# Matmuls on 64 by 32 array tiles issued in pairs, two PSUM tiles at a time, in a planned attention and SMELU kernel

## The chip, the cores and the metric

One core of one Trainium2 chip. The metric is device microseconds of one execution. The kernel before was timed three times: 260.14, 260.56 and 262.5 us, median 260.56.

## The reference

Two chained softmax attentions, then a two-layer network with a piecewise quadratic activation. Batch 8, 8 heads, 576 tokens, head size 64, 32 packed queries per head, d_ff 2048.

```python
def sm_attn(qq, kk, vv):
    s = scale * np.matmul(qq, kk.transpose(0, 1, 3, 2))
    s = s - np.max(s, axis=-1, keepdims=True)
    a = np.exp(s)
    a = a / (np.sum(a, axis=-1, keepdims=True) + 1e-09)
    return np.matmul(a, vv)
p_packed = sm_attn(p, k, v)
out = sm_attn(q, p_packed, p_packed)
...
h = x @ w_in
g = np.where(h >= 1, h, np.where(h <= -1, 0.0, (h + 1) ** 2 / 4))
return g @ w_out
```

## The kernel before

The work is split by batch b = 0 to 7; the output is made by pairs of batches, 1152 tokens in 9 tiles of 128 rows.

For each batch, `attention(b, key)` adds these steps. `trans` turns k and q: in batches 0 to 2 TensorE transposes them (`tp`, L359) and ScalarE or VectorE copies them into `kT` and `qT`; from batch 3 on `turned` (L479) does it with transposing transfers issued by SyncE, one for each half of the heads (parts 0 and 1). `scores` (`sp`, L387) multiplies kT with the packed queries pT, one PSUM tile for each half, and ScalarE takes the exponential (`ex`). `packed` (`pk`, L407 and L412) makes the packed values and their sums; they are copied into `ppT`. `weights(g, ...)` makes the second scores for one of two groups of heads: eight matmuls on 64 by 32 tiles of the array (`s`, L433, 288 columns), then exp (`eT`), sums over 32 rows by a matmul (`sm`, L443), ln and exp (`ln`, `rc`) and the product `A` (L454). `mk(f, ...)` makes a quarter of `M`, the packed values times w_in: eight matmuls on 64 by 32 tiles (`mp`, L473, 512 columns), copied out by ScalarE or VectorE.

Then `hidden_tile(b, fi)` (`h`, L513) multiplies M and A into a 128 by 576 tile, four matmuls, 16 tiles for each batch; ScalarE and VectorE apply the activation (`x`) and write `hT`. `out_tile(pr, i)` (`o`, L556) adds up 16 matmuls of 512 columns for each of the nine tiles of a pair; the result is copied to `ob` and SyncE writes it out (L562). All four kinds of engine work share 3 PSUM tiles ("W", `psW`), and o has 2 of its own ("O").

Nothing runs as it is written down. `Plan.run` is a list scheduler that runs when the kernel is built: each step has a cost for each engine (dictionary `C`), a key (its urgency), dependencies, and the PSUM room that it takes. For each engine `choose` takes the most urgent step that can start within half of the best candidate's cost after that candidate. The order that comes out is the program order of each engine. The plan's costs say 3.0 us for a load of k, q or v and 5.0 us for a transposing transfer. `mode` marks steps whose tiling of the array differs: 0 for the whole array, 1 for pk, 2 for s and mp; a step in another mode costs `switch` more.

SyncE's queue carries the transposing transfers and the output rows in one order. GpSimd's queue carries the loads; a load of k, q or v for batch b + 2 waits until the batch b buffer has been read.

Until the first output tiles, TensorE runs matmuls of zeros (L618) where the plan has a gap.

Of the kernel before, what the change touches and what calls it, by code (L numbers as in the profile page):

```python
# [9 lines left out]


C = dict(load=3.0, w_in=2.65, w_out=2.55, out=9.0, p=3.1, land=1.9, xt=5.0, xland=2.5,
         tpp=0.06, tp=0.042, sc=0.034, pk=1.18, s2=0.25, sm=0.245, M=0.345, h=0.49, o=0.217, switch=0.05,
         pTc=0.1, Tca=1.12, Tcd=0.76, Tc2a=0.64, Tc2d=0.457, ex=0.82, ppTa=0.26, ppTd=0.293, rs=0.18, eT=0.74, ln=0.65, rc=0.68, A=0.82,
         Mca=1.0, Mcd=1.22, x=0.65, ta=0.683, td=0.457, hT=0.758, oba=0.585, obd=0.69,
         array=0.2, wake=2.0, tell=0.04, feed=0.1, slack=0.6, margin=0.15, wait=0.5)
# [5 lines left out]
class Task:  # L22

    def __init__(self, engines, cost, key, deps, fn, takes, readers, frees, mode, slack, after, holds):
        self.engines, self.cost, self.key, self.deps, self.fn = engines, cost, key, list(deps), fn
        self.takes, self.readers, self.frees, self.mode = takes, readers, frees, mode
        self.slack, self.after, self.holds = slack, after, holds
        self.users, self.end, self.slot, self.gone = [], None, None, 0.0


class Plan:
# [15 lines left out]
    def add(self, engines, cost, key, deps, fn, takes=None, readers=0, frees=None, mode=None, slack=None, after=0.0,  # L47
            holds=0.0):
        engines = (engines,) if isinstance(engines, str) else engines
        t = Task(engines, cost if isinstance(cost, dict) else {e: cost for e in engines}, key, deps, fn, takes, readers,  # L50
                 frees, mode, slack, after, holds)
        t.seq = len(self.tasks)
        self.tasks.append(t)
        return t

    def ready(self, t, e):
        at = 0.0
        for d in t.deps:
            if e == "PE":
                lag = 0.0 if d.on == "PE" else C["feed"] + (C["margin"] if t.slack is None else t.slack)  # L60
            else:
                lag = C["array"] if d.on == "PE" else C["tell"] if d.on != e else 0.0
            at = max(at, d.end + lag)
        if t.takes:
            room = self.rooms[t.takes][self.count[t.takes] % len(self.rooms[t.takes])]
            if room is None:
                return None
            at = max(at, room + (C["feed"] if e == "PE" else 0.0))
        return at

    def choose(self, e, given, waiting):
# [37 lines left out]
    def run(self, idle):  # L109
        self.line = [t.seq for t in self.tasks if t.engines == ("DMA",)]  # L110
        left = {}
        given = {e: [] for e in self.ENGINES}
        for t in self.tasks:
            left[t] = len(t.deps)
            for d in t.deps:
                d.users.append(t)
            if not t.deps:
                for e in t.engines:
                    given[e].append(t)
        n = len(self.tasks)  # L120
        while n:
            best = None
            for e in self.ENGINES:
                c = self.choose(e, given, n)
                if c is not None and (best is None or c[0] < best[0]):
                    best = c[0], e, c[1]
            if self.count["O"] < 3:
                c, step = self.choose("PE", given, n), DW / 2400
                self.now["PE"] = max(self.now["PE"], C["wake"])
                if (c is None or c[0] > self.now["PE"] + step) and best is not None and best[0] > self.now["PE"]:  # L130
                    idle()
                    self.now["PE"] += step
                    continue
            assert best is not None
            at, e, t = best
            t.on = e
            cost = t.cost[e]
            if e == "PE" and t.mode is not None and t.mode != self.mode:
                cost += C["switch"]
                self.mode = t.mode  # L140
            self.now[e] = at + cost
            t.end = at + cost + t.after + (C["land"] if e == "DMA" else 0.0)
            if e == "DMA":
                del self.line[0]
            self.log.append((at, at + cost, e, t))
            if t.takes:
                room = self.rooms[t.takes]
                t.slot = self.count[t.takes] % len(room)
                room[t.slot] = None
                self.count[t.takes] += 1  # L150
                if t.readers == 0:
                    room[t.slot] = t.end + t.holds
            if t.frees is not None:
                f = t.frees
                f.gone = max(f.gone, t.end)
                f.readers -= 1
                if f.readers == 0:
                    self.rooms[f.takes][f.slot] = f.gone
            if len(t.engines) > 1:
                t.fn(e)  # L160
            elif e in ("ACT", "DVE"):
                t.fn(e)
            else:
                t.fn()
            for x in t.engines:
                given[x].remove(t)
            for u in t.users:
                left[u] -= 1
                if left[u] == 0:
                    for x in u.engines:  # L170
                        given[x].append(u)
            n -= 1
# [3 lines left out]
def kernel(  # L176
# [27 lines left out]
    G = 2  # L204
# [7 lines left out]
    FW = 512  # L212
    NF = d_ff // FW
# [56 lines left out]
    L = {}  # L270
# [31 lines left out]
    def both(fns, cost_a, cost_d, key, deps, **kw):  # L302

        return add((DVE, ACT), {ACT: cost_a, DVE: cost_d}, key, deps, fns, **kw)
# [35 lines left out]
    def attention(b, key):  # L340
# [36 lines left out]
        def scores(i, deps):  # L377
            box, ky = {}, key["sc" + str(i)]

            def mm():  # L380
                sp = box["sp"] = wide([P, 2, FW], f32, "sp")
                for j in range(2):
                    for e in range(E):
                        for g in range(G):
                            h, o = G * (2 * i + j) + g, (e * G + g) * X * NP
                            w = ((G * j + g) * E + e) * TP
                            nc.tensor.matmul(sp[:, j, o:o + X * NP], kT()[:, i, w:w + P],  # L387
                                             pT[:, b, h].rearrange("p x n -> p (x n)"), start=True, stop=True)

            def ev(eng):  # L390
                nc.scalar.activation(ex().rearrange("p e g x a n -> p a (e g x) n")[:, 2 * i:2 * i + 2],  # L391
                                     box["sp"][:TP, :, :E * G * X * NP].rearrange("p j (c n) -> p j c n", n=NP),
                                     AF.Exp, scale=scale)
            t = add(PE, C["sc"] * 12, ky, deps, mm, takes="W", readers=1, mode=0)
            return t, add(ACT, C["ex"], ky, [t] + old("pk"), ev, frees=t)

        def packed(deps):
            box, ky = {}, key["pk"]

            def mm():  # L400
# [9 lines left out]
                for g in range(G):  # L410
                    for c in range(NC):
                        nc.tensor.matmul(s_[:, g], ex_[:, c // X, g, c % X].rearrange("p a n -> p (a n)"), ones2[:TP],  # L412
                                         start=(c == 0), stop=(c == NC - 1))
            t = add(PE, C["pk"], ky, [L["v", b, 0]] + deps, mm, takes="W", readers=4, mode=1)
            war = old("s2", "M")
            res = [both(lambda eng: copy(ppT()[:, 0], box["v"])(eng), C["ppTa"], C["ppTd"], ky, [t] + war, frees=t)]
            for x in range(X):
# [8 lines left out]
        def weights(g, deps, r):  # L426
# [26 lines left out]
            def norm(eng):  # L453
                nc.vector.scalar_tensor_tensor(A()[:, g], box["eT"], rs()[:, g, :1], box["rc"], ALU.mult, ALU.mult)  # L454
            p_ = K.get((b - 1, "A" + str(g)), [])
            t = add(PE, C["s2"], ky, deps, mm, takes="W", readers=1, mode=2)
            e_ = add(ACT, C["eT"], ky, [t, r] + p_, exp2, frees=t)
            t2 = add(PE, C["sm"], km, [e_], mm2, takes="W", readers=1, mode=0)
            l_ = add(ACT, C["ln"], km, [t2] + last.get("ln", []), ln, frees=t2)
            i_ = add(ACT, C["rc"], km, [l_] + p_, inv)  # L460
            a_ = add(DVE, C["A"], km, [i_] + K.get((b - 2, "h"), []), norm)
            last["ln"] = [i_]
            K[b, "A" + str(g)] = [a_]
            return t, e_, a_

        def mk(f, deps):
            box, ky = {}, key["M" + str(f)]

            def mm():
                mp = box["mp"] = wide([P, G, FW], f32, "mp")  # L470
                for a in range(Q):
                    for g in range(G):
                        nc.tensor.matmul(mp[a * NP:(a + 1) * NP, g], pp_of(g, g, a),  # L473
                                         w_in_sb[g * D:(g + 1) * D, a, f * FW:(f + 1) * FW], start=True, stop=True)
            t = add(PE, C["M"], ky, deps + [L["in", f]], mm, takes="W", readers=1, mode=2)
            return t, both(lambda eng: copy(M()[:, :, f * FW:(f + 1) * FW], box["mp"])(eng),
                           C["Mca"], C["Mcd"], ky, [t] + K.get((b - 2, "h"), []), frees=t)

        def turned(nm, i, dst, prev):  # L479
            def go():  # L480
# [13 lines left out]
        pk, pc, r = packed([e0, e1])  # L494
        K[b, "sc"], K[b, "pk"] = [s0, s1], [pk]
        K[b, "kt"], K[b, "qt"] = [k0, k1], [q0, q1]
        ws = [weights(g, pc + qc0 + qc1, r) for g in range(G)]
        ms = [mk(f, pc) for f in range(NF)]
        K[b, "s2"], K[b, "M"] = [w[0] for w in ws], [m[0] for m in ms]
        K[b, "eT"], K[b, "A"] = [w[1] for w in ws], [w[2] for w in ws]  # L500
        K[b, "Mc"] = [m[1] for m in ms]
# [147 lines left out]
```

## Time and profile before

| what | value |
|---|---|
| median of three runs | 260.56 us |
| profiled execution | 261.9 us, span 259.8 us |
| TensorE busy | 247.3 us, 95% |
| VectorE / ScalarE busy | 173.3 us, 67% / 185.9 us, 72% |
| HBM read / written | 37.22 MB / 9.44 MB |
| mean granted TensorE clock | 0.995 |

The span runs from the first to the last instruction. PE is TensorE, PEld its weight loads, ACT ScalarE, DVE VectorE, POOL GpSimd, SP SyncE; a q behind a name is the engine's sequencer, which issues transfers. In a list in order of time a row gives the start, the time from the first start to the last end, the line, what is written and read, and the number of instructions; in square brackets stands the idle time before it and what ended it. In the table by stretches of time the columns are the stretch, its length, then busy time and number of instructions of PE, PEld, DVE, ACT and POOL, the granted clock, the share of the DMA engines and GB/s. A landing row gives the time from a transfer's issue to its landing.

### The profile page before, as it was taken

Reading aid. Unit: us, or ns where it says so; the run is one execution under the profiler, and the core shown is the slowest. Engines: PE = TensorE matmul, PEld = TensorE weight load, DVE = VectorE, ACT = ScalarE, POOL = GpSimd, SP = SyncE. Lnnn points to the kernel's source line nnn. Section 1 sums busy time; section 2 is a strip of 40 time slices with the busy share of each in tenths; the row PEclk is TensorE's granted clock in tenths of the full one; section 3 lists DMA queues with packets and bytes.
Section 4 is the critical chain, followed back from the end, with each engine's and each line's share of the span. In section 5 each row is a group of like instructions: output and inputs, shape, how many; then the busy total and the mean of one; then the engine's idle time right before and its main releaser. Section 6 shows DMA issues by size and latency. Waiting matters only on the chain.

```text
span 259.8 us, 5951 instructions
## 1 busy us (share of the span) xinstructions
PE 247.3 (95%) x2432; PEld 145.7 (56%) x2466; DVE 173.3 (67%) x299; ACT 185.9 (72%) x303; POOL 27.4 (11%) x40
## 2 busy tenths in 40 slices
PE   7999989999998999999999999999999999999992
PEld 5978546467545655654655565555554465644440
DVE  5135989678988997999748974897268876940000
ACT  3447886789898898999949895998559775841110
POOL 8522312102100300210201000000000000000000
PEclk9999999999999999999999999999999999999997
DMA  7999999999999999999999995301222111133223
GB/s 108 187 204 206 208 202 195 217 230 194 139 148 196 148 226 183 178 164 179 161 165 141 154 217 122 76 19 31 43 81 43 42 43 40 40 78 85 59 63 82
DMA packets 54764, 34.40 MB, mean 132 GB/s; under 512 B 27473, under 2 KB 50257, under 8 KB 54737
## 3 DMA queue, kind: packets, MB, share of 16 engines
q0 software_dynamic: 24608, 18.55, 51.7%
q1 hardware_dynamic: 29968, 15.34, 33.4%
q8 instruction: 19, 0.31, 0.5%
q10 hardware_dynamic: 160, 0.13, 0.2%
q14 instruction: 9, 0.07, 0.1%
HBM read 37.22 MB, written 9.44 MB: 180 GB/s over the span
## 4 chain that ended last, share of the span: by engine, by line
PE 70%; DMA 20%; ACT 5%; issue 2%; POOL 1%; SPq 0%; DVE 0%; POOLq 0%
PE o L556 41%; PE h L513 17%; DMA k<-in_k_dram 8%; DMA kT<-k 6%; DMA w_in_sb<-in_moe_w_in_dram 5%; PE mp L473 2%; PE pk L407 2%; ACT eT L438 2%; PE sp L387 2%; PE tp L359 2%; ACT x L518 1%; ACT M L307 1%; PE pk L412 1%; PE s L433 1%; DMA out_dram<-ob 1%
## 5 line engine op out<-in xcount | busy, mean ns | idle before, releaser
L556 PE MATMUL o<-w_out_sb,hT 128*128 128x512 bf16 x542 | 136.2, 379 | 1.3 <-issue 0.5
L528 DVE SCALAR_TENSOR_TENSOR hT<-x 128x576 bf16<-128x576 f32 x128 | 94.2, 756 | 22.3 <-PE o L556 16.4
L518 ACT ACTIVATE x<-h 128x576 f32<-128x576 f32 x128 | 78.9, 658 | 11.3 <-PE h L513 7.4
L556 PEld LDWEIGHTS <-hT 128*128 128x128 bf16 x576 | 54.6, 98 | 54.4 <-issue 4.3
L513 PE MATMUL h<-A,M 128*128 128x288 bf16 x512 | 78.5, 286 | 1.5 <-ACT M L307 0.7
L513 PEld LDWEIGHTS <-M 128*128 128x128 bf16 x512 | 48.4, 98 | 25.6 <-issue 3.6
L523 DVE TENSOR_SCALAR x<-x 128x576 f32<-128x576 f32 x102 | 47.0, 463 | 13.7 <-ACT x L518 12.8
L307 ACT COPY ob<-o 128x512 f32<-128x512 f32 (+1 forms) x24 | 13.8, 576 | 36.7 <-PE o L556 36.1
L307 DVE COPY ob<-o 128x512 f32<-128x512 f32 (+1 forms) x13 | 8.7, 668 | 27.2 <-ACT ob L307 24.9
L307 ACT CAST M<-mp 128x1024 bf16<-128x1024 f32 x26 | 25.9, 1011 | 0.0
L618 PE MATMUL o<-zeros 128*128 128x256 bf16 x138 | 18.3, 285 | 1.2 <-DVE zeros L242 1.2
L525 ACT ACTIVATE x<-x 128x576 f32<-128x576 f32 x26 | 17.5, 684 | 0.5
L618 PEld LDWEIGHTS <-zeros 128*128 128x128 bf16 x138 | 13.5, 102 | 3.7 <-DVE zeros L242 1.2
L454 DVE SCALAR_TENSOR_TENSOR A<-eT,rs,rc 128x576 bf16<-128x576 bf16 x16 | 13.0, 814 | 2.5 <-ACT rc L451 2.3
L391 ACT ACTIVATE ex<-sp 96x768 bf16<-96x768 f32 x16 | 12.9, 815 | 2.3 <-PE sp L387 2.3
L254 POOL DMA_DIRECT2D k<-in_k_dram x9 | 7.4, 821 | 67.8 <-issue 28.7
L473 PE MATMUL mp<-w_in_sb,ppT 64*32 64x512 bf16 x256 | 13.1, 384 | 0.9 <-ACT x L518 0.4
L438 ACT ACTIVATE eT<-s,rs 128x576 bf16<-128x576 f32 x16 | 11.7, 744 | 1.1 <-PE s L433 0.9
L447 ACT ACTIVATE ln<-sm 128x576 f32<-128x576 f32 x16 | 10.5, 657 | 1.2 <-PE sm L443 1.1
L451 ACT ACTIVATE rc<-ln 128x576 f32<-128x576 f32 x16 | 10.9, 684 | 0.5
L387 PEld LDWEIGHTS <-kT 128*128 128x128 bf16 x192 | 7.6, 98 | 3.3 <-DMA kT<-k 1.3
L307 ACT CAST ppT<-pk 64x128 bf16<-64x128 f32 (+1 forms) x21 | 5.4, 259 | 5.6 <-PE pk L412 4.5
(44 smaller groups left out, 116.2 us busy)
## 6 DMA issues: line engine op xcount, KB each, us to landing
q<-in_q_dram POOLq DMA_DIRECT2D x8, 576.0 KB, 15.3
v<-in_v_dram POOLq DMA_DIRECT2D x8, 576.0 KB, 16.1
out_dram<-ob SPq DMA_DIRECT2D x23, 192.0 KB, 2.8
k<-in_k_dram POOLq DMA_DIRECT2D x7, 576.0 KB, 14.7
out_dram<-ob SPq DMA_DIRECT2D x24, 128.0 KB, 2.4
w_in_sb<-in_moe_w_in_dram POOLq DMA_DIRECT2D x4, 512.0 KB, 18.3
w_out_sb<-in_moe_w_out_dram POOLq DMA_DIRECT2D x4, 512.0 KB, 19.1
out_dram<-ob SPq DMA_DIRECT2D x23, 64.0 KB, 2.2
```

Source lines behind the costliest of these rows:

```text
L307: return lambda eng: nc.vector.tensor_copy(out_, in_) if eng == DVE else nc.scalar.copy(out_, in_)
L391: nc.scalar.activation(ex().rearrange("p e g x a n -> p a (e g x) n")[:, 2 * i:2 * i + 2], box["sp"][:TP, :, :E * G * X * NP].rearrange("p ...
L438: nc.scalar.activation(box["eT"], box["s2"][:, :, :HALF], AF.Exp, scale=rs()[:, g, 1:])
L454: nc.vector.scalar_tensor_tensor(A()[:, g], box["eT"], rs()[:, g, :1], box["rc"], ALU.mult, ALU.mult)
L473: nc.tensor.matmul(mp[a * NP:(a + 1) * NP, g], pp_of(g, g, a), w_in_sb[g * D:(g + 1) * D, a, f * FW:(f + 1) * FW], start=True, stop=True)
L513: nc.tensor.matmul(h[:, hf, :HALF], T[b, "M"][:, g, fi * P:(fi + 1) * P], T[b, "A"][:, g, hf], start=(g == 0), stop=(g == G - 1))
L518: nc.scalar.activation(box["x"], box["h"][:, :, :HALF], AF.Prelu, bias=-1.0, alpha=0.5)
L523: nc.vector.tensor_scalar(x, x, 1.0, 0.0, ALU.add, ALU.max)
L525: nc.scalar.activation(x, x, AF.Relu, bias=1.0)
L528: nc.vector.scalar_tensor_tensor(hT[:, fi, col:col + S].rearrange("p (a t) -> p a t", a=2), box["x"], 1.0, box["x"], ALU.min, ALU.mult)
L556: nc.tensor.matmul(box["o"], hT[:, fi, i * P:(i + 1) * P], w_out_sb[:, fi, :], start=(fi == 0), stop=(fi == KF - 1))
L618: plan.run(lambda: nc.tensor.matmul(o[:, :DW], zeros[:, :P], zeros[:, :DW], start=True, stop=True))
```

## The change

From batch 1 on, the steps of `weights` and `mk` no longer add their TensorE part themselves. They yield it, and a new function `tiled` joins two of them into one step that takes two PSUM tiles at once: the second scores of group 0 with the first quarter of M, those of group 1 with the second, and the third quarter with the fourth. In batch 0 each stays a step of its own. A step may now take several PSUM tiles, each with its own readers.

The plan's rules change as well. `switch` goes from 0.05 to 0.09 and is charged only on the way into a mode other than 0; a joined step costs 0.11 less than its parts (`join`); and after a step of over 0.4 us on ScalarE or VectorE the engine counts as free 0.085 us earlier (`lap`). Some steps get further dependencies: scores on the pk of batch b - 2, pk on its s, M and A, M on its h, and the second scores on A of batch b - 1.

```diff
-         ... o=0.217, switch=0.05,
+         ... o=0.217, switch=0.09, lap=0.085, join=0.11,
...
         if t.takes:
-            room = self.rooms[t.takes][self.count[t.takes] % len(self.rooms[t.takes])]
-            if room is None:
-                return None
-            at = max(at, room + (C["feed"] if e == "PE" else 0.0))
+            rooms = self.rooms[t.takes]
+            for j in range(len(t.readers)):
+                room = rooms[(self.count[t.takes] + j) % len(rooms)]
+                if room is None:
+                    return None
+                at = max(at, room + (C["feed"] if e == "PE" else 0.0))
...
-                cost += C["switch"]
+                cost += C["switch"] if t.mode else 0.0
                 self.mode = t.mode
-            self.now[e] = at + cost
+            self.now[e] = at + cost - (C["lap"] if e in ("ACT", "DVE") and cost > 0.4 else 0.0)
...
-            t = add(PE, C["sc"] * 12, ky, deps, mm, takes="W", readers=1, mode=0)
+            t = add(PE, C["sc"] * 12, ky, deps + old("pk"), mm, takes="W", readers=1, mode=0)
...
-            t = add(PE, C["pk"], ky, [L["v", b, 0]] + deps, mm, takes="W", readers=4, mode=1)
+            t = add(PE, C["pk"], ky, [L["v", b, 0]] + deps + old("s2", "M", "A"), mm, takes="W", readers=4, mode=1)
...
-            t = add(PE, C["s2"], ky, deps, mm, takes="W", readers=1, mode=2)
-            e_ = add(ACT, C["eT"], ky, [t, r] + p_, exp2, frees=t)
+            t, j = yield ky, C["s2"], deps + p_, mm
+            e_ = add(ACT, C["eT"], ky, [t, r] + p_, exp2, frees=(t, j))
...
-            t = add(PE, C["M"], ky, deps + [L["in", f]], mm, takes="W", readers=1, mode=2)
-            return t, both(lambda eng: copy(M()[:, :, f * FW:(f + 1) * FW], box["mp"])(eng),
-                           C["Mca"], C["Mcd"], ky, [t] + K.get((b - 2, "h"), []), frees=t)
+            t, j = yield ky, C["M"], deps + [L["in", f]] + K.get((b - 2, "h"), []), mm
+            yield t, both(lambda eng: copy(M()[:, :, f * FW:(f + 1) * FW], box["mp"])(eng),
+                           C["Mca"], C["Mcd"], ky, [t] + K.get((b - 2, "h"), []), frees=(t, j))
+
+        def tiled(*units):
+            units = list(units)
+            asked = [next(u) for u in units]
+            t = add(PE, sum(a[1] for a in asked) - C["join"] * (len(asked) - 1), asked[0][0], [d for a in asked for d in a[2]],
+                    lambda: [a[3]() for a in asked], takes="W", readers=[1] * len(units), mode=2)
+            return [u.send((t, j)) for j, u in enumerate(units)]
...
-        ws = [weights(g, pc + qc0 + qc1, r) for g in range(G)]
-        ms = [mk(f, pc) for f in range(NF)]
+        ws, ms = [weights(g, pc + qc0 + qc1, r) for g in range(G)], [mk(f, pc) for f in range(NF)]
+        if b == 0:
+            ws, ms = [tiled(w)[0] for w in ws], [tiled(m)[0] for m in ms]
+        else:
+            pairs = [tiled(w, m) for w, m in zip(ws, ms)] + [tiled(*ms[2:])]
+            ws, ms = [p_[0] for p_ in pairs[:2]], [p_[1] for p_ in pairs[:2]] + pairs[2]
```

More of the change, by code (lines that the diff above doesn't have):

```diff
@@ L12 @@
 C = dict(load=3.0, w_in=2.65, w_out=2.55, out=9.0, p=3.1, land=1.9, xt=5.0, xland=2.5,
-         tpp=0.06, tp=0.042, sc=0.034, pk=1.18, s2=0.25, sm=0.245, M=0.345, h=0.49, o=0.217, switch=0.05,
+         tpp=0.06, tp=0.042, sc=0.034, pk=1.18, s2=0.25, sm=0.245, M=0.345, h=0.49, o=0.217, switch=0.09, lap=0.085, join=0.11,
          pTc=0.1, Tca=1.12, Tcd=0.76, Tc2a=0.64, Tc2d=0.457, ex=0.82, ppTa=0.26, ppTd=0.293, rs=0.18, eT=0.74, ln=0.65, rc=0.68, A=0.82,
@@ L25, in __init__ @@
         self.engines, self.cost, self.key, self.deps, self.fn = engines, cost, key, list(deps), fn
-        self.takes, self.readers, self.frees, self.mode = takes, readers, frees, mode
-        self.slack, self.after, self.holds = slack, after, holds
-        self.users, self.end, self.slot, self.gone = [], None, None, 0.0
+        self.takes, self.readers = takes, list(readers) if isinstance(readers, (list, tuple)) else [readers]
+        self.frees = (frees, 0) if isinstance(frees, Task) else frees
+        self.mode, self.slack, self.after, self.holds = mode, slack, after, holds
+        self.users, self.end, self.slots, self.gone = [], None, None, [0.0] * len(self.readers)
 class Plan:
@@ L147, in run @@
                 room = self.rooms[t.takes]
[L148 to L152, printed above, removed]
-            if t.frees is not None:
[L154 to L158, printed above, removed]
+                t.slots = [(self.count[t.takes] + j) % len(room) for j in range(len(t.readers))]
+                self.count[t.takes] += len(t.slots)
+                for n_, j in zip(t.readers, t.slots):
+                    room[j] = None if n_ else t.end + t.holds
+            if t.frees is not None:
+                f, j = t.frees
+                f.gone[j] = max(f.gone[j], t.end)
+                f.readers[j] -= 1
+                if f.readers[j] == 0:
+                    self.rooms[f.takes][f.slots[j]] = f.gone[j]
             if len(t.engines) > 1:
@@ L463, in weights @@
             K[b, "A" + str(g)] = [a_]
-            return t, e_, a_
+            yield t, e_, a_
         def mk(f, deps):
```

## Prediction

> **What bounds the kernel now.** I read the head of the page, then TensorE in order of time, then SyncE's own list of transfers, and last what the scores waited for.
>
> ```profile
> span 259.8 us, 5951 instructions
> PE 247.3 (95%) x2432; PEld 145.7 (56%) x2466; DVE 173.3 (67%) x299; ACT 185.9 (72%) x303; POOL 27.4 (11%) x40
> ...
> PE 70%; DMA 20%; ACT 5%; issue 2%; POOL 1%; SPq 0%; DVE 0%; POOLq 0%
> ...
> L556 PE MATMUL o<-w_out_sb,hT 128*128 128x512 bf16 x542 | 136.2, 379 | 1.3 <-issue 0.5
> ...
> L513 PE MATMUL h<-A,M 128*128 128x288 bf16 x512 | 78.5, 286 | 1.5 <-ACT M L307 0.7
> ```
>
> TensorE is busy 95% of the span, and the chain that ended last is 70% PE and 20% DMA. The DMA share sits in the first third. So there are two clocks: TensorE's stream, and the arrival of transposed k and q for batches 3 to 7, which SyncE issues. TensorE runs in program order, so a matmul placed ahead of its transfer stops everything behind it.
>
> The pitch of each kind, and what it costs to go into the 64 by 32 tiles and out again, come from stretches in which TensorE did not wait:
>
> ```profile
> 88.28 2.10 PE L556 MATMUL o<-w_out_sb,hT 128*128 128x512 bf16 x9
> ...
> 90.90 0.60 PE L556 MATMUL o<-w_out_sb,hT 128*128 128x512 bf16 x2
> ...
> 98.64 0.65 PE L513 MATMUL h<-A,M 128*128 128x288 bf16 x4
> 99.23 0.41 PE L473 MATMUL mp<-w_in_sb,ppT 64*32 64x512 bf16 x8
> 99.57 0.66 PE L513 MATMUL h<-A,M 128*128 128x288 bf16 x4
> ...
> 109.78 0.38 PE L556 MATMUL o<-w_out_sb,hT 128*128 128x512 bf16 x1
> ...
> 111.27 1.14 PE L513 MATMUL h<-A,M 128*128 128x288 bf16 x8
> ...
> 138.44 1.67 PE L556 MATMUL o<-w_out_sb,hT 128*128 128x512 bf16 x7
> ...
> 140.50 0.66 PE L513 MATMUL h<-A,M 128*128 128x288 bf16 x4
> 141.00 0.38 PE L556 MATMUL o<-w_out_sb,hT 128*128 128x512 bf16 x1
> ...
> 141.56 0.82 PE L556 MATMUL o<-w_out_sb,hT 128*128 128x512 bf16 x3
> ...
> 146.35 2.97 PE L556 MATMUL o<-w_out_sb,hT 128*128 128x512 bf16 x13
> ```
>
> The second column is first start to last end, and one matmul lasts 379 ns (o) or 286 ns (h). So o has a pitch of (2.97 - 0.38) / 12 = 0.216 us and h of (1.14 - 0.29) / 7 = 0.122. A lone quarter of M: the four h from 98.64 have streamed by 99.13, the next h starts at 99.57, so it costs 0.44, though its eight matmuls run side by side for about one o pitch; the other 0.22 is the way in and out. In the same manner a lone s costs 0.345 (141.00 + 0.216 to 141.56), the row s, M costs 0.55 (138.44 + 7 x 0.216 to 140.50), the row s, M, s costs 0.68 (88.28 + 9 x 0.216 to 90.90), and the pk group 1.27 (109.78 + 0.216 to 111.27).
>
> **The change part by part.** The number of matmuls stays (576 o, 512 h, 128 s, 256 M). What changes is how they are grouped, and, because the plan now counts an overlap of 0.085 us between steps of ScalarE and VectorE and has new dependencies, the whole order.
>
> Grouping. In the order before, batches 1 to 7 enter the 64 by 32 tiles 34 times. Batches 1, 5, 6 and 7 have (s, M), s and three lone M: 0.55 + 0.345 + 3 x 0.44 = 2.215 each. Batch 2 has two s and four M alone: 2.45. Batches 3 and 4 have (s, M, s) and three M: 2.0 each. In all 15.3 us. Afterwards each has (s, M) twice and (M, M): 21 entries. No row shows (M, M). It lies between a lone M plus one pitch, 0.44 + 0.216 = 0.65, and two lone ones, 0.88; I take 0.65, since the second half of a row is shown to cost only its stream ((s, M) less s is 0.205). That is 7 x (1.10 + 0.65) = 12.25. The change takes 3.1 us off TensorE (1.5 with the other end).
>
> Order. I laid the two programs' instruction lists side by side. The hidden tiles and output steps that stood ahead of the scores (sp) now stand behind them. SyncE's list hardly changes: the half transposes of k and q keep their places among the output tiles. This is what the gain runs into:
>
> ```profile
> 58.87 1.54 SPq L481 DMA_TRANSPOSE kT<-k  x1
> 61.39 0.79 SPq L562 DMA_DIRECT2D out_dram<-ob  x2
> 62.32 5.59 SPq L481 DMA_TRANSPOSE qT<-q  x1
> 67.97 8.43 SPq L481 DMA_TRANSPOSE kT<-k  x1
> ```
> ```profile
> 60.04 1.03 PE L556 MATMUL o<-w_out_sb,hT 128*128 128x512 bf16 x4
> ...
> 83.82 0.52 PE L387 MATMUL sp<-pT,kT 128*128 128x64 bf16 x12 [0.79 <-DMA kT<-k]
> ...
> 129.73 0.51 PE L387 MATMUL sp<-pT,kT 128*128 128x64 bf16 x12
> ```
> ```profile
> 67.97 15.81 DMA kT<-k
> ```
>
> The 61.39 issue is output tile 3; its last matmul is the second of the four at 60.04, so 60.26. Behind it on SyncE stand a q half and the second k half of batch 3, which lands 15.81 us after its issue, at 83.8. The second half of batch 3's scores (sp) came to it at 83.03 and waited 0.79 us.
>
> Step 1, batch 3. Between that matmul of tile 3 and this half of the scores TensorE had 31 o, 72 h, six groups of s or M and the rest: about 20.9 us of work, done in 22.8. In the changed program 24 o (5.2), 40 h (4.9), one pk group (1.3), two (s, M) (1.1), four sums (0.5) and twelve scores (0.35, pitch 0.029 from the 0.52 us row) stand there: 13.3 us. With the same 1.9 us of small waits it arrives at 60.3 + 15.2 = 75.5. Work ahead of tile 3's end is about equal in both orders, so I keep 60.3. The transposition sits behind the same q load and shares the queues with the same loads of batch 4, so I keep its landing, 83.8. A wait of 0.8 becomes one of 8.3 us; its ends are 0 and 10.5, without small waits. All behind it on TensorE waits too. From here to the end the changed program has 7 o and 24 h more (1.5 + 2.9) and 1.25 less of grouping: it ends 3.2 us later than before, from this one wait.
>
> Step 2, batch 5. The same arrangement returns with output tile 7:
>
> ```profile
> 103.33 1.18 SPq L562 DMA_DIRECT2D out_dram<-ob  x2
> 104.61 1.55 SPq L481 DMA_TRANSPOSE qT<-q  x1
> 106.22 6.49 SPq L481 DMA_TRANSPOSE kT<-k  x1
> ...
> 142.91 8.60 SPq L481 DMA_TRANSPOSE kT<-k  x2
> ```
> ```profile
> DMA to landing us min/median/max: 18.3/18.3/18.3
> ```
> ```profile
> DMA to landing us min/median/max: 5.8/7.8/9.7
> ```
>
> The first landing row is that of the k half at 106.22 alone (124.5 us), the second that of the two at 142.91, when no other loads were in the way. From 83.8 TensorE now needs 40 o, 72 h, a pk group, two (s, M), one (M, M), sums and scores to finish tile 7: 21.6 us, at 105.4; its copy and issue took 61.39 - 60.26 = 1.1, so 106.5. Before, 21.2 us went from this issue to the landing (103.33 to 124.5): 127.7. With empty queues it would be 1.3 + 1.6 + 9.7 behind the issue: 119.1. TensorE itself comes to the second half of batch 5's scores after 61 o, 128 h, two pk groups, three (s, M), two (M, M), four sums and 48 scores, 36.2 us: at 120.0. So the wait is between 0 and 7.7 us. I take 125, nearer the loaded end, because the loads of batch 6 are released by the half before it, as now. Behind it the changed program has 427 o against 384 (+9.3), 256 h against 232 (+2.9), four sums (+0.5) and 6.45 against 6.65 of grouping: 12.5 more than followed 129.73 before. The end moves by 125 + 12.5 - 129.7 = +7.8 us. This holds step 1 and the gain of the grouping.
>
> Step 3, runs of hidden tiles. Here ScalarE's pace counts:
>
> ```profile
> 103.15 2.88 ACT L518 ACTIVATE x<-h 128x576 f32<-128x576 f32 x5
> ```
>
> It starts one every (2.88 - 0.65) / 4 = 0.558 us, while TensorE makes one in 0.49. The new order has runs of 24 to 32 h without an o between (before, mostly 4 to 12). Three find a free PSUM tile, each further one waits 0.07: behind batch 5's scores 23 of them, +1.6 us. Its ends are 0, if waits elsewhere give the rooms back, and 23 x 0.16 = 3.7, at ScalarE's undiminished 0.65.
>
> Step 4, the clock after a wait.
>
> ```profile
> 1.20 2.74 PE L618 MATMUL o<-zeros 128*128 128x256 bf16 x12 [1.20 <-DVE zeros L242]
> ```
> ```profile
> 240.00:260.00 20.00, 14.95 (x69) 6.61 (x68) 0.42 (x1) 2.72 (x5) 0.00 (x0) 0.93 0.27 69
> ```
>
> The first twelve idle matmuls take (2.74 - 0.29) / 11 = 0.22 us for 256 columns, where o takes 0.216 for 512: a cold array runs at half pace, which cost about 12 x 0.11 = 1.3 us. The last window's clock of 0.93 shows that it falls again within the 5 us after the last matmul. An 8 us wait can do the same. After step 1 this only shortens step 2's wait; after step 2 it costs 0 to 1.3. I take 0 and leave the rest to the range. The Trainium skill (TensorE: Matmul & The Clock Gate, Part 1) says that an idle window of about 3.4 us halves the clock until as long a busy one has passed, which gives an estimate of 1.7 us for each long wait. By that page the upper end would be 0.4 us higher for each.
>
> Batch 7's first k half stands behind output tile 12, with 22 o, 32 h and 24 scores (9.4 us) between on TensorE; 1.1 + 1 + 9.7 us on the other side make a wait of up to 2.4 us, which goes to the upper end only.
>
> Sum: +7.8 + 1.6 = +9.4 us. The profiled execution took 261.9 us, 2.1 of it outside the span of 259.8, and would take 271.3. It stood 1.3 above the median of 260.56, so against the median the forecast is **270.0 us**.
>
> **Rivals.** (a) The transposes are there in time, and only the grouping counts: -3.1 us, 257.5. For it: transposition alone took 5.8 to 9.7 us, and loads of batch 4 can start earlier. Against it: the second half of batch 3 would have to land by 75.5, 8.3 us sooner, with a q half of 5.59 us still ahead of it; above 79 or so (75.5 + 3.1, plus the little that follows) the gain is gone. (b) Only step 1 bites, batch 5's half landing by 120: +3.2, 263.8. For it, step 2's interval is half made of other loads' traffic. (c) A pair takes two of three PSUM tiles, and h finds one left:
>
> ```profile
> 76.64 0.41 PE L473 MATMUL mp<-w_in_sb,ppT 64*32 64x512 bf16 x8 [0.45 <-ACT x L518]
> ```
>
> If each of 21 groups waits 0.45 like this one for its rooms, and the transposes do not bite: 21 x 0.45 - 3.1 = +6.4, 267. Against it, one such row in a whole trace. The Trainium skill (TensorEngine Tiling (Array Packing), PSUM Bottleneck) says that after tiling the copies out of PSUM may become the bound; that speaks for (c), and this row is all the trace has of it. (d) The joined groups drain between their two tiles all the same and nothing waits longer: 260.6.
>
> **How the numbers follow.** Forecast 0.58, (a) 0.12, (b) 0.15, (c) 0.08, (d) 0.04, and 0.03 for worse than all of it. The forecast's own range: down to 120.0 + 12.5 - 129.7 = +2.8 (263.4); up to 127.7 + 12.5 - 129.7 + 3.7 + 1.3 + 2.4 less overlaps of 2, about +16 (276). The range 262 to 276 leaves out (a), (d) and the worst, not quite 0.2. Faster by over 1% (some 2.6 us, about what a measurement here tells from no change) is 0.10, most of (a); within 1% is 0.06, the rest of (a) and (d); slower 0.84.
>
> **What would show it.** Steps 1 and 2 right: the rows of sp with a wait of 6 us or more at about 76 to 84 us, and of 2 to 7 at about 120 to 127, released by kT. Grouping right: 21 groups in batches 1 to 7, (s, M) at 0.55 and (M, M) at 0.65. Step 3: waits for ACT x in runs of h. Step 4: a clock below 0.99. The prediction is wrong if the second half of batch 3's scores runs before 79 us, or if batch 5's follows without a wait and the end lies below 262.

## The result, and the profile after

The change is slower: 269.26 us median (268.85 to 270.19), before 260.84 in the same comparison, ratio 1.0309, interval 1.0274 to 1.0345. The forecast was 270.0. The ratios here and below leave disturbed executions out, the medians do not. Each ratio is against the kernel before as timed alongside, with medians of 260.84 to 261.85. The profiled execution has a span of 266.9 us, 7.1 more than before.

The page's head and the same two groups of the changed kernel:

```profile
span 266.9 us, 5977 instructions
PE 252.3 (95%) x2465; PEld 146.8 (55%) x2465; DVE 176.6 (66%) x298; ACT 181.6 (68%) x304; POOL 27.1 (10%) x40
...
L572 PE MATMUL o<-w_out_sb,hT 128*128 128x512 bf16 x576 | 140.1, 382 | 0.3 <-DVE hT L544 0.2
...
L529 PE MATMUL h<-A,M 128*128 128x288 bf16 x512 | 75.5, 288 | 0.8 <-DVE rs L424 0.8
```

TensorE is 95% busy in both, which tells nothing here: a matmul at half clock counts as busy too (the four h at 82.24 below take 1.17 us, those at 107.44 take 0.67). TensorE in order of time shows more:

```profile
49.76 0.67 PE L363 MATMUL tp<-ident,k 96*128 96x96 bf16 x12 [1.51 <-ACT pT L311]
...
75.56 0.51 PE L391 MATMUL sp<-pT,kT 128*128 128x64 bf16 x12 [0.17 <-ACT x L534]
81.20 0.82 PE L391 MATMUL sp<-pT,kT 128*128 128x64 bf16 x12 [5.13 <-DMA kT<-k]
...
82.24 1.17 PE L529 MATMUL h<-A,M 128*128 128x288 bf16 x4
...
86.34 0.63 PE L477 MATMUL mp<-w_in_sb,ppT 64*32 64x512 bf16 x16
...
105.07 1.89 PE L572 MATMUL o<-w_out_sb,hT 128*128 128x512 bf16 x8
106.89 0.63 PE L477 MATMUL mp<-w_in_sb,ppT 64*32 64x512 bf16 x16
107.44 0.67 PE L529 MATMUL h<-A,M 128*128 128x288 bf16 x4
...
116.23 2.61 PE L529 MATMUL h<-A,M 128*128 128x288 bf16 x20 [0.80 <-DVE rs L424]
...
121.80 0.51 PE L391 MATMUL sp<-pT,kT 128*128 128x64 bf16 x12
...
230.73 31.46 PE L572 MATMUL o<-w_out_sb,hT 128*128 128x512 bf16 x145
```

The joined group does what it should: (M, M) costs 0.64 us (105.07 + 8 x 0.216 to 107.44). But the second half of batch 3's scores, first half at 75.56, waits 5.13 us for kT, and what follows runs slowly. The stretches of time show why; the third column from the right is the granted clock:

```profile
60.00:80.00 20.00, 15.90 (x194) 9.32 (x192) 18.91 (x33) 15.13 (x26) 1.55 (x2) 0.98 1.32 177
80.00:100.00 20.00, 18.77 (x201) 10.53 (x202) 14.07 (x24) 15.11 (x26) 2.44 (x3) 0.85 1.18 184
```

A mean of 0.85 over 20 us is 6 us at half clock, and 0.98 before it 0.8 us more; taken by single microseconds the granted clock is 0.50 throughout from 80 to 86 us. The last o starts at 230.73 + 31.46 - 0.38 = 261.8, before at 254.6.

SyncE's issue of the halves of k, batch 3's second and batch 5's second, and where each landed (12.3 and 6.4 us after its issue, in this order):

```profile
68.85 6.70 SPq L493 DMA_TRANSPOSE kT<-k  x1
...
110.28 2.36 SPq L493 DMA_TRANSPOSE kT<-k  x1
```
```profile
DMA to landing us min/median/max: 12.3/12.3/12.3
```
```profile
DMA to landing us min/median/max: 6.4/6.4/6.4
```

### The profile page after: what moved, and what is told of

Same layout as the page of the kernel before. It is cut to its first block, busy times and chain, and to the rows that moved or that the text cites. A ratio compares the mean times of both kernels' runs of the same rounds, so it can differ in the third digit from the quotient of the medians.

```text
span 266.9 us, 5977 instructions
## 1 busy us (share of the span) xinstructions
PE 252.3 (95%) x2465; PEld 146.8 (55%) x2465; DVE 176.6 (66%) x298; ACT 181.6 (68%) x304; POOL 27.1 (10%) x40
## 4 chain that ended last, share of the span: by engine, by line
PE 73%; DVE 12%; DMA 9%; ACT 2%; issue 2%; POOL 1%; SPq 0%; DVEq 0%; ACTq 0%; POOLq 0%
PE o L572 41%; PE h L529 18%; DVE hT L544 7%; DMA kT<-k 5%; DMA v<-in_v_dram 4%; DVE x L539 3%; PE mp L477 2%; PE pk L411 2%; PE o L634 2%; PE sp L391 2%; PE tp L363 1%; PE sm L447 1%; DVE M L311 1%; PE pk L416 1%; PE s L437 1%
## 5 line engine op out<-in xcount | busy, mean ns | idle before, releaser
L572 PE MATMUL o<-w_out_sb,hT 128*128 128x512 bf16 x576 | 140.1, 382 | 0.3 <-DVE hT L544 0.2
L534 ACT ACTIVATE x<-h 128x576 f32<-128x576 f32 x128 | 76.5, 652 | 16.9 <-PE h L529 14.4
L529 PE MATMUL h<-A,M 128*128 128x288 bf16 x512 | 75.5, 288 | 0.8 <-DVE rs L424 0.8
L539 DVE TENSOR_SCALAR x<-x 128x576 f32<-128x576 f32 x88 | 40.4, 460 | 12.0 <-ACT x L534 10.8
L311 ACT COPY ob<-o 128x512 f32<-128x512 f32 (+1 forms) x28 | 16.2, 578 | 43.4 <-PE o L572 43.1
L541 ACT ACTIVATE x<-x 128x576 f32<-128x576 f32 x40 | 26.9, 688 | 0.4
L311 DVE COPY ob<-o 128x512 f32<-128x512 f32 (+1 forms) x9 | 5.8, 657 | 27.1 <-ACT ob L311 26.0
L311 DVE CAST M<-mp 128x1024 bf16<-128x1024 f32 x16 | 19.5, 1221 | 2.9 <-PE mp L477 2.9
L311 ACT CAST M<-mp 128x1024 bf16<-128x1024 f32 x16 | 16.0, 1014 | 0.1
L391 PE MATMUL sp<-pT,kT 128*128 128x64 bf16 x192 | 8.5, 196 | 5.4 <-DMA kT<-k 5.1
```

What stands on the lines that cost most here:

```text
L311: return lambda eng: nc.vector.tensor_copy(out_, in_) if eng == DVE else nc.scalar.copy(out_, in_)
L529: nc.tensor.matmul(h[:, hf, :HALF], T[b, "M"][:, g, fi * P:(fi + 1) * P], T[b, "A"][:, g, hf], start=(g == 0), stop=(g == G - 1))
L534: nc.scalar.activation(box["x"], box["h"][:, :, :HALF], AF.Prelu, bias=-1.0, alpha=0.5)
L539: nc.vector.tensor_scalar(x, x, 1.0, 0.0, ALU.add, ALU.max)
L541: nc.scalar.activation(x, x, AF.Relu, bias=1.0)
L572: nc.tensor.matmul(box["o"], hT[:, fi, i * P:(i + 1) * P], w_out_sb[:, fi, :], start=(fi == 0), stop=(fi == KF - 1))
```

## The experiments

In the table, overlap is the constant `lap`, and landing in the plan is `xland`, what the plan adds to the 5.0 us of a transposing transfer until its data can be used. Rival R is case (c) of the prediction: a pair holds two of three PSUM tiles and starves the hidden tiles. Rival P says that the plan's new constants and dependencies are to blame, not the pairs or the transfers.

| run | pairs | overlap | landing in the plan | other | median us | ratio to before | interval |
|---|---|---|---|---|---|---|---|
| change | yes | 0.085 | 2.5 | | 269.26 | 1.0309 | 1.0274 to 1.0345 |
| e1 | no | 0.085 | 2.5 | | 265.61 | 1.0136 | 1.0093 to 1.0179 |
| e2 | yes | 0.085 | 12.0 | | 262.75 | 1.0036 | 1.0013 to 1.0060 |
| e3 | yes | 0.085 | 2.5 | idle at most 1/4 | 267.35 | | |
| e4 | yes | 0.085 | 12.0 | idle at most 1/4 | 259.34 | 0.9882 | 0.9815 to 0.9949 |
| e5 | yes | 0.085 | 2.5 | a q half left out | 267.87 | 1.0252 | 1.0219 to 1.0285 |
| e6 | yes | 0.085 | 2.5 | TensorE kept busy | 267.28 | 1.0231 | 1.0202 to 1.0260 |
| e7 | no | 0 | 2.5 | | 260.69 | 0.9992 | 0.9957 to 1.0026 |
| e8 | yes | 0 | 12.0 | | 258.34 | 0.9882 | 0.9851 to 0.9914 |
| e9 | yes | 0 | 2.5 | | 271.82 | 1.0396 | 1.0361 to 1.0432 |

**e1, the pairs undone.**

```diff
-        if b == 0:
+        if b >= 0:
             ws, ms = [tiled(w)[0] for w in ws], [tiled(m)[0] for m in ms]
```

> The change with its pairs undone: each second score and each quarter of M is a step of its own again, while the plan's new constants and dependencies stay. Theory (the new order brings the scores of batch 3 ahead of their transposed k, and the rest follows from that wait): between the end of output tile 3 and the second half of batch 3's scores this order again has 20.3 us of work (20.9 before, 13.3 in the change), so a wait under 2 us, no cold clock, and none of the 3 us of grouping: 260 to 262 us. Rival R (a pair takes two of three PSUM tiles and starves the hidden tiles): no pairs, so about 261 too. Rival P (the plan's new constants and dependencies make the worse order by themselves): 267 us or more, with the wait for kT still there.

Measured 265.61 us, ratio 1.0136: outside every range expected, and a miss for the theory that the one wait explains all. The wait for kT is down to 0.41 us. Another is there, and the clock fell after it:

```profile
50.42 0.32 PE L437 MATMUL s<-qT,ppT 64*32 64x288 bf16 x8 [1.94 <-ACT pT L311]
```
```profile
40.00:60.00 20.00, 17.78 (x254) 10.54 (x255) 10.91 (x17) 14.54 (x22) 2.31 (x3) 0.91 1.37 214
```

So rival P has a part of the loss, one that is there without the pairs.

**e2, the transposes land later in the plan.**

```diff
-         xt=5.0, xland=2.5,
+         xt=5.0, xland=12.0,
```

> The change, with one number of the plan altered: a transposing transfer is taken to land 12.0 us after its issue instead of 2.5. The pairs, and all else, stay. Theory: the scores of batch 3 move back behind 20.6 us of work after output tile 3, the wait of 5.1 us and the cold clock behind it (about 2.4 us) go, the grouping's 3 us come out, and the longer runs of hidden tiles cost about 1: 258 to 260 us. Rival R: the pairs hold the PSUM tiles as before, 266 to 269. Rival P: 266 to 269.

Measured 262.75 us, ratio 1.0036. The transfers take what they take; only the plan's belief was altered, and with it TensorE's order. It gave back 6.5 us with all pairs kept, which rivals R and P had excluded. No score waits for kT any more (their 0.5 us of idle time is for ScalarE):

```profile
L529 PE MATMUL h<-A,M 128*128 128x288 bf16 x512 | 75.2, 285 | 2.2 <-ACT ppT L311 0.8 <-ACT x L534 0.7 <-DVE rs L424 0.3
...
L391 PE MATMUL sp<-pT,kT 128*128 128x64 bf16 x192 | 8.3, 193 | 0.5 <-ACT x L534 0.4
```

It stayed 2.75 us above the upper end: h now waits for PSUM tiles and ScalarE, and a wait of 1.51 us for pT near 50 us, the place of e1's, is still there. Whether the overlap constant is behind both is left to e8.

**e3, less idling for urgent steps.**

```diff
-         margin=0.15, wait=0.5)
+         margin=0.15, wait=0.25)
```

> The change, with another number of the plan altered: TensorE may idle for a more urgent step by a quarter of the other step's cost instead of half, so an o is put between hidden tiles where the next would wait 0.07 us. The scores of batch 3 still come after only 14.3 us of work behind output tile 3. Theory: the wait for kT (4 to 5 us) and the cold clock stay, the small waits in runs of hidden tiles (1.6 to 2.7 us) go: 266 to 268 us. Rival R: 268 to 270, nothing of it depends on the runs. If the runs cost nothing: 269.

Measured 267.35 us as a median, but its four executions go from 261.63 to 267.96, so that it can't be counted for the theory's range of 266 to 268. The profiled one, of 267.86 us, waits elsewhere than I said:

```profile
81.98 0.52 PE L391 MATMUL sp<-pT,kT 128*128 128x64 bf16 x12 [0.29 <-DMA kT<-k]
...
102.91 0.82 PE L391 MATMUL sp<-pT,kT 128*128 128x64 bf16 x12 [4.90 <-DMA kT<-k]
```

Batch 4's second half, not batch 3's, meets its transfer late. Which one depends on where this order puts each half; what the runs of hidden tiles cost can't be read from it. Inconclusive for step 3.

**e4, both.**

```diff
-         xt=5.0, xland=2.5,
+         xt=5.0, xland=12.0,
...
-         margin=0.15, wait=0.5)
+         margin=0.15, wait=0.25)
```

> Both alterations of the plan, pairs kept: transposing transfers land 12.0 us after issue, and TensorE idles by at most a quarter of a step's cost. Theory: no wait for kT, no cold clock, no long runs of hidden tiles: the grouping's gain stands alone, 257 to 258.5 us, faster than both kernels. Rival R: 266 to 269. Rival P: 266 to 269.

Measured 259.34 us, ratio 0.9882: faster than both kernels, with a median 0.84 us above the range. Both rivals are out for this order. Two of its four executions, 258.12 and 258.25, lie in the range; the others took 260.44 and 264.98. The longest is the one profiled and waits 3.3 us for a half of kT near 152 us; what the others waited for is not on record.

**e5, the same order with one transfer less.** The first half of q of batch 3 isn't transposed.

```diff
         def turned(nm, i, dst, prev):
             def go():
+                if (b, nm, i) == (3, "q", 0):
+                    return
```

> The change in its own TensorE order, with one transposing transfer left out: the first half of q of batch 3, which stands on SyncE ahead of the second half of k (batch 3's second scores then read an older qT in that half, at the same cost). Theory: the k half is issued about 5 us sooner and lands before TensorE asks for it at 75.9 us, or within 1 us of it; the wait of 5.1 us and the cold clock behind it (2.5 us) go: 261.5 to 264 us. Rival P (the order is bad by many small waits, whatever lands when): 267 to 269. If the half then lands only 2 us sooner because other traffic holds it: 266.

Measured 267.87 us, ratio 1.0252: a miss. The k half was issued at once in the q half's place:

```profile
64.43 4.90 SPq L495 DMA_TRANSPOSE kT<-k  x1
```
```profile
DMA to landing us min/median/max: 16.0/16.0/16.0
```
```profile
80.46 0.52 PE L391 MATMUL sp<-pT,kT 128*128 128x64 bf16 x12 [3.68 <-DMA kT<-k]
```

It was issued 4.4 us sooner and landed at 80.4 instead of 81.2. So its place in SyncE's queue does not set the landing. What does is open. The loads of batch 4, in transit in the same stretch, are the likely cause: in all three traces the half lands within 1.0 us of batch 4's v (83.8 and 83.2 before, 81.1 and 80.2 in the change, 80.4 and 80.8 here). Taking those loads away was not tried.

**e6, TensorE kept busy in the wait.**

```diff
                 sp = box["sp"] = wide([P, 2, FW], f32, "sp")
+                if (b, i) == (3, 1):
+                    for _ in range(48):
+                        nc.tensor.matmul(sp[:, 0, :DW], zeros[:, :P], zeros[:, :DW], start=True, stop=True)
```

> The change with 48 matmuls of zeros (256 columns, about 5.2 us) put into the PSUM tile of the second half of batch 3's scores, ahead of its real matmuls, so that TensorE is busy while it waits for kT; the wait itself stays. Theory (the clock falls to half in the wait and costs 2.5 us behind it): 266 to 267.5 us, and no stretch of half clock near 80 us. If the clock costs nothing that something else does not cost anyway: 269 to 270.

Measured 267.28 us, ratio 1.0231 against 1.0309 for the change: 0.8%, 2 us. From the second half of the scores to the next group of M it takes 2.71 us (81.53 to 84.24), in the change 5.14 (81.20 to 86.34):

```profile
76.29 5.40 PE L388 MATMUL sp<-zeros 128*128 128x256 bf16 x48
81.53 0.51 PE L394 MATMUL sp<-pT,kT 128*128 128x64 bf16 x12
...
84.24 0.62 PE L480 MATMUL mp<-w_in_sb,ppT 64*32 64x512 bf16 x16
```
```profile
80.00:100.00 20.00, 19.60 (x229) 12.18 (x227) 15.84 (x27) 16.34 (x29) 2.43 (x3) 1.00 1.23 179
```

The second half of the scores starts no earlier than before, and the clock is 1.00 throughout. The half clock costs 2.4 us, shown apart from the wait that causes it. The Trainium skill (TensorE: Matmul & The Clock Gate, Part 1) states a window of about 3.4 us for the fall and for the return, from which one window at half clock would cost an estimated 1.7 us. The trace of the change has more because its 6.8 us of half clock are twice that window.

**e7, no pairs and no overlap.** The edit of e1, and

```diff
-         switch=0.09, lap=0.085, join=0.11,
+         switch=0.09, lap=0.0, join=0.11,
```

> No pairs, and the plan's overlap of 0.085 us set to 0; the switch cost of 0.09 and the new dependencies stay. It splits what e1 lost. Theory now (the overlap makes the plan too tight: it leaves TensorE waiting about 2 us for copies of pT near 50 us, after which the clock falls once): the order is nearly that before, 260.5 to 262. If the new dependencies or the switch cost did it: 264 to 266.

Measured 260.69 us, ratio 0.9992: the same as before. So e1's loss came from the overlap constant; the dependencies and the switch cost, which are still in, make none without it.

**e8, pairs, no overlap, late landing in the plan.** The change and

```diff
-         xt=5.0, xland=2.5,
+         xt=5.0, xland=12.0,
...
-         switch=0.09, lap=0.085, join=0.11,
+         switch=0.09, lap=0.0, join=0.11,
```

> Pairs kept, overlap 0, transposing transfers taken to land 12.0 us after issue. Theory: scores stand behind 22.8 us of work after output tile 3, near 96, 119.5 and 146 us of work for batches 4 to 6, late enough for every transfer; no wait near 50 us and no cold clock; the grouping's gain of 2.6 us of TensorE work comes out whole: 257 to 259 us, without the scatter of the last run. Rival R (pairs starve the hidden tiles of PSUM): 263 or more.

Measured 258.34 us (257.59 to 258.56), ratio 0.9882: as the theory said, faster than both kernels. Against e2 the overlap constant alone was changed, and it is worth some 4 us here; no wait for pT is left near 50 us. Hidden tiles and scores hardly wait, though every pair holds two PSUM tiles, so rival R is out:

```profile
L529 PE MATMUL h<-A,M 128*128 128x288 bf16 x512 | 78.1, 286 | 0.4 <-ACT x L534 0.4
```
```profile
98.45 0.51 PE L391 MATMUL sp<-pT,kT 128*128 128x64 bf16 x12
...
105.42 0.51 PE L391 MATMUL sp<-pT,kT 128*128 128x64 bf16 x12
```

These are both halves of batch 4, without a wait.

**e9, pairs and no overlap, landing as in the change.**

```diff
-         switch=0.09, lap=0.085, join=0.11,
+         switch=0.09, lap=0.0, join=0.11,
```

> Pairs kept, overlap 0, transposing transfers taken to land 2.5 us after issue as in the change: with the runs before it fills the table of overlap and landing for the pairs. Its order has 22.8 us of work between output tile 3 and the second half of batch 3's scores, so no wait there, but it asks for batch 4's second half after 90.5 us of work and for batch 6's after 116.2, where the version with a landing of 12.0 does so after 96.3 and 146.0. Theory (the plan's landing time decides whether pairs gain or lose, by scores put ahead of their transfers): waits for kT at batch 4 (2 to 5 us) and above all at batch 6 (8 to 15 us, its k cannot be there before some 135 to 142 us), each with a fall of the clock: 268 to 276 us. If the overlap alone made the change slow: 258 to 260.

Measured 271.82 us, ratio 1.0396, with waits at both batches named. The second, which is for the first half of batch 6, is shorter than I said:

```profile
101.61 0.52 PE L391 MATMUL sp<-pT,kT 128*128 128x64 bf16 x12 [2.61 <-DMA kT<-k]
...
129.32 0.82 PE L391 MATMUL sp<-pT,kT 128*128 128x64 bf16 x12 [5.74 <-DMA kT<-k]
```
```profile
120.00:140.00 20.00, 13.82 (x175) 7.54 (x176) 8.97 (x17) 9.48 (x15) 1.80 (x2) 0.74 1.34 186
```

Against e7 only the pairs are added, and they cost about 11 us: the pairs alone are enough to bring the scores ahead of their transfers under the plan's landing of 2.5 us. With 12.0 the same pairs gain (e8). Taking the overlap out did not help here: the change itself had 269.26.

## Why the prediction was right, and where it was not

The mechanism was right in its first step: the new order asks for transposed k before it is there. The second step, a longer wait at batch 5, did not happen. In its waits the run is rival (b), in which only step 1 bites, and (b) had +3.2 us, which would be about +0.5 with the half landing 2.65 us sooner, as it did. The rest of the measured +7.2 is the clock, the runs of hidden tiles, a wait for rs and small losses, for which the forecast had 1.6 in all. So that 270.0 came out within 0.7 us is in good part luck. By the prediction's own signs, the wait at batch 3 is short of 6 us, the one at batch 5 is missing and no run of hidden tiles shows a wait for x; the groups and the clock (0.987) are as it said.

- Grouping, -3.1 us: right as far as the rows show it. (M, M) measured 0.64 for the 0.65 taken. With the scores out of the transfers' way, the change with pairs comes to 258.34 us (e8), where rival (a) had 257.5; without pairs 260.69 (e7), in which the plan's landing differs too, so no run isolates the total.
- Step 1, batch 3: right in place; 5.13 us of wait where 8.3 was forecast. TensorE came at 76.1 (81.20 less 5.13; forecast 75.5), by two misses that mostly cancel: the last matmul of tile 3 started at 61.8 and not at 60.3 (the wait for pT lies ahead of it), and the small waits on the way were 0.9 us and not 1.9. The term that was mis-sized is the landing, kept at 83.8: it was 68.85 + 12.3 = 81.15. The loads of batch 4, which the prediction took to be the same, came earlier in the new order: its v had landed at 80.2, before at 83.2. They do not share a queue with the half, as the prediction has it: GpSimd's queue issues them, and SyncE's the half.
- Step 2, batch 5: wrong. There was no wait. The half landed 6.4 us after its issue, not 18.3, at 116.7, and TensorE came at 121.80. The forecast had carried over an interval measured in other traffic; the lower end of its range, no wait, is what came. In the order before, the half landed with batch 6's v, at 124.5 and 124.7; in the new one that load was issued only at 114.14. The forecast had 125 for this point, 3.2 too much.
- Step 3: the runs of hidden tiles after batch 5's scores lost less than forecast. The run of 32, and two others like it, by the same list:

```profile
130.00 4.21 PE L529 MATMUL h<-A,M 128*128 128x288 bf16 x32
...
146.24 3.44 PE L529 MATMUL h<-A,M 128*128 128x288 bf16 x24
...
215.64 3.67 PE L529 MATMUL h<-A,M 128*128 128x288 bf16 x28
```

  Less 0.29 and a pitch of 0.122 for each, they lose 0.1, 0.3 and 0.1 us; all six together 1.1, where 1.6 was forecast. The whole way from 121.80 to the last o took 140.0 us, 1.0 more than forecast (124.9 + 12.5 + 1.6).
- Step 4, the clock: its cost was taken as 0, on the ground that step 1's part would vanish in step 2's wait. Step 2's wait did not come, and the 2.4 us stood (e6).
- Not foreseen: the 1.51 us wait for copies of pT and the 0.80 for rs. A wait of 1.51 to 1.94 us for pT near 50 us stands in the traces of all seven kernels with the overlap of 0.085 us and in none of the three with 0. e1 and e7 show that this overlap makes an order that is 1.4% slower even without pairs. The prediction named it as one reason for the new order and gave it no price. In the change the wait for pT lies ahead of the one for kT, which would have been longer without it, had the transfer landed at the same time.

Put together for the profiled execution: the second half of batch 3's scores starts 2.6 us sooner than before (81.20 against 83.82). From there to the last o the change takes 180.6 us against 170.8, 9.8 more. Of these, 3.2 are the work that the prediction counted, the grouping's gain taken off; 2.4 are the clock, 1.1 the runs, 0.8 the wait for rs, and 2.3 are small losses that no row singles out. That makes +7.2 at the last o, where the forecast had +9.4.

In the forecast's own terms the profiled execution would take 271.3 us; it took 268.85, so the sum was 2.4 too high. The median is met more closely because the execution profiled before stood 1.3 us above its median, and that of the change 0.4 below.

## What to carry to other kernels

When steps on an in-order engine become cheaper or are regrouped, list what each of them waits for, and count the work between a transfer's trigger and its consumer in the old order and in the new: 20.9 us against 13.3 told this result. The planner here believes that a transposed half lands 7.5 us after it starts (5.0 + 2.5), where 3.4 to 18.3 were measured in the two traces; with the order before that cost 0.79 us of waiting for kT, with the pairs 5.13. Raising this one cost (the landing, e9 to e8) took off some 13 us, more than the 3.1 us that the grouping can gain. The cost that describes an engine's overlap did harm without pairs (e1 against e7) and with pairs and the late landing (e2 against e8), but not in the change itself (e9, without it, is over 2 us slower): the worth of one constant depends on the others.

## What was not expected of the hardware

A wait of 1.94 us on TensorE was followed by half clock (e1, 0.91 over 20 us, 3.6 us of it); the 1.51 us in the change was not (1.00 in the same stretch), and neither was the 2.61 us of e9 at 101.61. The length of a wait alone does not tell, then. The rows of the change and of e9:

```profile
40.00:60.00 20.00, 18.39 (x283) 11.69 (x282) 13.48 (x21) 14.81 (x23) 3.09 (x4) 1.00 1.36 218
```
```profile
100.00:120.00 20.00, 18.18 (x197) 11.02 (x202) 16.24 (x27) 15.43 (x28) 3.20 (x4) 1.00 1.25 189
```

And one transposing transfer of the same size landed 6.4 to 18.3 us after its issue in two kernels that issue it in the same place of the same queue.
